# Leftover tokens of a routed mixture of experts: counting moved one batch earlier, x turned by 32x32 blocks on VectorE, their x read at the start of the last batch

## Chip, cores and metric

One core of one Trainium2 chip. The metric is the device time in microseconds (us), and the median of the runs is compared.

## The reference

Pooled attention feeds a mixture of experts in two levels. What is computed, cut to what matters:

```python
k_p = k.reshape(B, H, Sp, 8, D).mean(axis=3); v_p = v.reshape(B, H, Sp, 8, D).mean(axis=3)
attn = softmax(q @ k_p.T / sqrt(D)) @ v_p              # B=8, H=8, S=576, D=64, Sp=72
x = attn.transpose(0, 2, 1, 3).reshape(B * S, H * D)   # 4608 tokens of 512
g_idx = argmax(x @ w_group)                            # one of 4 groups, its softmax weight g_w
e_idx = argmax(x @ w_expert[g_idx])                    # one of 4 experts of it, weight e_w
out = g_w * e_w * (relu(x @ w1[g, e]) @ w2[g, e])      # w1 512x1024, w2 1024x512, float32
```

## The kernel before, in words

The kernel goes through the 8 batches one after another. Nearly all tokens of a batch choose the same expert. So each batch elects its main expert, and all its 576 tokens go through that expert; the gate of a token that chose another one is zero. Those few others, the **leftovers**, are done at the end in blocks of up to 32 slots, one expert to a block. The first block is written into the order of the last batch, and a loop behind it runs once for every further block (none in this execution).

The order of the work is written out by hand in strings, one per stage: START, FIRST (batch 0), SECOND (batch 1), STEADY (batches 2 to 6) and LAST (batch 7). Each word is one piece, and each engine takes its own instructions in the order of the words. `m.` is the expert product of the batch itself, `n.` the attention and routing of the next batch, `w.` the next batch's weights, `l.` the leftovers. The engines meet only at semaphores, which the framework places where a tile is written, read or handed on.

* `m.up:f:h` (line 602) is one slice of x @ w1 for half h of the tokens: 12 matmuls on TensorE into one of three PSUM banks (pool ps_m), and a relu on ScalarE (line 604). `m.upd` (lines 610, 615) is the VectorE part that takes the low half of the result and sets the bank free. So slice k waits for the `upd` of slice k-3.
* `m.down:z` (lines 631, 642, 663) is 8 matmuls of h @ w2. Three of these make a chunk of 128 tokens, which ScalarE scales and stores (line 636).
* `load`, `cast`, `lo` bring in a quarter of w1 (1:0 to 1:3) or of w2 (2:0 to 2:3): a DMA on SyncE's queue (line 573) into one of four buffers (pool sw), a rounding on ScalarE (line 579) and the remainder on GpSimd, or on VectorE where the word ends in `:v` (line 585). The buffer comes free after `lo`.
* `n.xlo` (line 418) is a GpSimd subtraction over x. `n.keep_x` (line 555) writes x to the DRAM tile xscr if the batch has leftovers.
* `l.step` advances the generator `place` (19 pieces) that counts the leftovers. Piece 1 makes a triangle and two constants, pieces 2 to 5 are one matmul each (line 733) into a bank of ps_t (pool of three) with a VectorE copy out of it (line 734), and the rest is short VectorE work (lines 738 to 771).
* `l.which` (lines 778 to 785) finds batch and expert of a block and has SyncE read both into registers. `l.slots` (lines 793 to 810) and `l.rows` (lines 816 to 818) find the tokens. `l.xtiles` clears two tiles on GpSimd (line 824), `l.fetch_x` (line 834), `l.fetch_a` and `l.fetch_b` read x and the expert's weights.
* `l.whole` (line 848) adds the high and low parts of x, by chunks of 128 tokens, on VectorE or GpSimd. `l.turn` (lines 858, 859) transposes a chunk on TensorE and copies it out. `l.gather` (line 866) picks the 32 tokens by a matmul with a one-hot matrix, `l.back` (line 872) transposes the result. `l.up`, `l.hback`, `l.down` (lines 880 to 899) are the expert on 32 tokens and the scattered store.

In STEADY the words that touch batches 8 and later do nothing. In batch 6, the last to use it, it ends with

```python
m.down:0 n.rt:1 x.kr:0 m.down:1 n.route m.down:2 x.kr:1 z.load_k m.down:3 m.down:4 n.main_expert w.load:1:0 w.load:1:1 w.load:1:2 w.load:1:3 m.down:5
x.qb:0 n.gates n.gm_ n.xlo:1 n.keep_x m.down:6 x.kt m.down:7 x.sc:0 x.mx:0 x.sd:0 w.cast:1:0 w.lo:1:0 w.load:2:0 m.down:8 x.ex:0 x.qb:1 w.cast:1:1 w.load:2:1 m.down:9
x.su_:0 x.nm:0:p w.lo:1:1 m.down:10 m.down:11 m.down:12 w.cast:1:2 m.down:13 w.cast:1:3
```

Of the kernel before, what the change touches and what calls it, by code (L numbers as in the profile page):

```python
# [68 lines left out]
m.load:2:3 m.load:2:2 m.up:0:0 p.tail m.upd:0:0 m.lo:1:2:v m.up:0:1 l.step m.upd:0:1 m.up:1:0 l.step l.step m.upd:1:0 m.up:1:1 l.step l.step m.upd:1:1 l.xtiles  # L69
m.up:2:0 m.cast:2:1 l.step m.upd:2:0 l.step m.up:2:1 l.step m.upd:2:1 l.step m.up:3:0 l.step l.step m.upd:3:0 m.up:3:1 l.step l.step m.upd:3:1  # L70
m.up:5:0 l.step l.step l.step l.step m.upd:5:0 m.lo:1:3 m.cast:2:2 m.up:4:0 l.step l.step l.which m.lo:2:2:v m.upd:4:0 m.lo:2:1:v
m.up:6:0 m.cast:2:0 m.upd:6:0 m.up:5:1 m.lo:2:0:v m.up:4:1 m.up:6:1 m.cast:2:3 l.fetch_x l.tiles m.upd:5:1 m.upd:4:1 m.upd:6:1 l.slots m.down:0 m.down:1 l.fetch_a:1
# [7 lines left out]
def attn_moe(ctx: ExitStack, tc: tile.TileContext, q, k, v, wg, we, w1, w2, out):  # L80
    nc = tc.nc
    tt, ts, stt = nc.vector.tensor_tensor, nc.vector.tensor_scalar, nc.vector.scalar_tensor_tensor
# [602 lines left out]
    class Left:  # L685
# [22 lines left out]
        def place(s):  # L708
# [13 lines left out]
            s.sl = [sl[:, 128 * c:128 * c + 128] for c in range(NC)]  # L722
            s.xg, s.xs, s.h = sl[:, 640:768], sl[:, 768:896], sl[:, 896:1152]
            s.hT = sl[:, 1152:1408].rearrange("p (t x) -> p t x", t=2)
            s.y = sl[:, 1408:1536]
# [94 lines left out]
        def xtiles(s):  # L820
            s.xh = [pp.tile([128, 5, S], F32, name="pT")[:, 0:NG], xp.tile([128, NG, S], F32, name="xr")]

            for t in s.xh:
                nc.gpsimd.memset(t, 0.0)
# [21 lines left out]
        def whole(s, c):  # L846
            o, n = CH[c]
            (nc.gpsimd if c % 2 else nc.vector).tensor_tensor(
                out=s.xh[0][:, :, o:o + n], in0=s.xh[0][:, :, o:o + n], in1=s.xh[1][:, :, o:o + n], op=ALU.add)

        def turn(s, c):

            if s.xr is None:
                s.xr = xp.tile([128, 2, 4, 320], F32, name="xb").rearrange("p i g s -> p (i g s)").rearrange("p (c x) -> p c x", c=NC)
            o, n = CH[c]
            ps = ps_t.tile([128, 512], F32, name="tp")
            for g in range(4):
                nc.tensor.transpose(out=ps[0:n, 128 * g:128 * g + 128], in_=s.xh[0][:, g, o:o + n], identity=ident)
            (nc.vector.tensor_copy if c % 2 else nc.scalar.copy)(out=s.xr[0:n, c, :], in_=ps[0:n])

        def gather(s):

            ps = ps_t.tile([128, 512], F32, name="tp")
            for c, (o, n) in enumerate(CH):
                for g in range(4):
                    nc.tensor.matmul(ps[32 * g:32 * g + BS, 0:128], lhsT=s.sl[c][0:n, 0:BS], rhs=s.xr[0:n, c, 128 * g:128 * g + 128],
                                     start=(c == 0), stop=(c == NC - 1))
            nc.scalar.copy(out=s.xg, in_=ps[:, 0:128])
# [132 lines left out]
```

## Time and profile before

| | us |
|---|---|
| median of 3 runs | 515.48 (514.2 to 516.41) |
| the profiled execution, its own time | 514.15 |
| its span in the trace | 512.4 |

How to read the rows further down. A row of a timeline has start, duration, engine, line, operation, output<-input, shape and how many instructions were merged; brackets tell how long the engine had been idle and what released it. PE is TensorE (PEld its weight loads), DVE VectorE, ACT ScalarE, POOL GpSimd, SPq the DMA issues of SyncE. A row of the chain has start, duration and what the end of the program hung on just then. One float32 matmul gives two instructions, a transpose one.

### The profile page before, as it was taken

What the parts mean: (1) busy time and instruction counts of PE and PEld (TensorE: products, weight loads), DVE (VectorE), ACT (ScalarE), POOL (GpSimd) and SP (SyncE); (2) the same over time, 40 slices, a digit from 0 to 9 for tenths busy, and PEclk for the clock granted to TensorE, in tenths of its full rate; (3) what the DMA queues carried; (4) which work ended last, traced back from release to release, by engine and by line L of the source; (5) the groups of instructions that cost most, each with busy time, mean ns of one, the idle gap of its engine ahead of it and who ended that gap; (6) DMA issues with size and microseconds to landing.
All of it is one profiled execution on the core that took longest, in us unless ns stands there. A gap on an engine that the chain in (4) does not pass through costs nothing.

```text
span 512.4 us, 14902 instructions
## 1 busy us (share of the span) xinstructions
PE 501.1 (98%) x6085; PEld 440.1 (86%) x6085; DVE 345.6 (67%) x928; ACT 206.3 (40%) x385; POOL 281.6 (55%) x246
## 2 busy tenths in 40 slices
PE   8899999999999999999999999999999999998996
PEld 6688987998889978899789988899789988898976
DVE  6876877899385869486784768476784764199702
ACT  2354432545216542455216551455325551344212
POOL 2386666576518595476828585476947471830400
PEclk9799999999999999999999999999999999999999
DMA  8699299685428966954197615985055100923751
GB/s 279 191 260 205 24 280 236 124 192 137 77 92 242 265 106 176 318 150 80 29 308 213 151 26 138 368 311 89 1 191 192 43 3 22 304 96 114 271 172 58
DMA packets 118110, 83.70 MB, mean 163 GB/s; under 512 B 71034, under 2 KB 93818, under 8 KB 117784
## 3 DMA queue, kind: packets, MB, share of 16 engines
q1 hardware_dynamic: 113408, 75.67, 54.7%
q10 hardware_dynamic: 4600, 7.02, 4.0%
q8 instruction: 49, 0.80, 0.7%
q14 instruction: 21, 0.17, 0.1%
q0 software_dynamic: 32, 0.04, 0.0%
HBM read 77.28 MB, written 28.53 MB: 206 GB/s over the span
## 4 chain that ended last, share of the span: by engine, by line
PE 76%; DVE 10%; DMA 5%; ACT 2%; POOL 2%; issue 2%; SPq 1%; ACTq 0%; DVEq 0%; POOLq 0%
PE mm L602 30%; PE mm L631 27%; PE mm L642 4%; PE sc L396 4%; PE sc L336 4%; DMA vv<-in_v_dram 2%; DMA sw<-in_moe_w_dram 2%; PE tp L429 1%; PE mm L663 1%; POOL w L585 1%; DVE s L368 1%; DVE ht L615 1%; DVE pT L382 1%; PE tp L425 1%; DVE p L357 1%
## 5 line engine op out<-in xcount | busy, mean ns | idle before, releaser
L631 PE MATMUL mm<-w,ht 128*128 128x512 f32 x744 | 172.6, 385 | 0.0
L585 POOL TENSOR_TENSOR w<-sw,w 128x1024 fp32r<-128x1024 f32 (+2 forms) x86 | 145.2, 1711 | 33.7 <-ACT w L579 29.2
L631 PEld LDWEIGHTS mm<-w,ht 128*128 128x128 f32 x744 | 136.8, 189 | 25.2 <-issue 6.4
L602 PE MATMUL mm<-xb,w 128*128 128x288 f32 (+1 forms) x768 | 109.6, 294 | 1.7 <-DVE ht L610 1.7
L602 PEld LDWEIGHTS mm<-xb,w 128*128 128x128 f32 x768 | 100.7, 189 | 6.1 <-ACT w L579 2.2
L602 PE MATMUL mm<-xa,w 128*128 128x288 f32 (+1 forms) x768 | 100.2, 283 | 0.5 <-ACT xa L401 0.5
L602 PEld LDWEIGHTS mm<-xa,w 128*128 128x128 f32 x768 | 95.5, 190 | 2.2 <-ACT xa L401 0.9
L604 ACT ACTIVATE ht<-mm 128x288 fp32r<-128x288 f32 (+2 forms) x128 | 51.9, 410 | 87.1 <-PE mm L602 85.4
L375 POOL TENSOR_TENSOR p<-p,su 128x864 f32<-128x864 f32 (+2 forms) x30 | 40.3, 1343 | 78.6 <-DVE su L370 67.7
L579 ACT CAST w<-sw 128x1024 fp32r<-128x1024 f32 x64 | 66.7, 1042 | 31.5 <-DMA sw<-in_moe_w_dram 29.0
L615 DVE SCALAR_TENSOR_TENSOR ht<-mm,ht 128x64 fp32r<-128x64 f32 (+4 forms) x192 | 37.7, 252 | 25.8 <-ACT ht L604 25.5
L636 ACT ACTIVATE y<-mm,gm 128x512 f32<-128x512 f32 x31 | 21.2, 684 | 66.4 <-PE mm L631 66.4
L362 ACT ACTIVATE p<-p 128x864 f32<-128x864 f32 (+2 forms) x30 | 23.4, 780 | 37.5 <-DVE p L357 29.6
L368 DVE TENSOR_REDUCE s<-p 128x12 f32<-128x864 f32 (+2 forms) x30 | 25.8, 861 | 15.1 <-ACT p L362 15.1
L382 DVE STREAM_TRANSPOSE pT<-p 128x960 f32<-128x960 f32 (+2 forms) x30 | 29.2, 972 | 8.0 <-POOL p L375 7.2
L610 DVE SCALAR_TENSOR_TENSOR ht<-mm,ht 128x288 fp32r<-128x288 f32 (+1 forms) x64 | 26.9, 422 | 10.4 <-ACT ht L604 10.4
L642 PE MATMUL mm<-w,ht 128*128 128x512 f32 x128 | 29.5, 381 | 0.0
L336 PEld LDWEIGHTS sc<-kT,qT 64*32 64x32 f32 x2176 | 23.7, 105 | 6.3 <-issue 3.5
L336 PE MATMUL sc<-kT,qT 64*32 64x72 f32 x2176 | 28.5, 229 | 0.5 <-DVE qT L322 0.2
L675 DVE TENSOR_TENSOR y<-mm,y 64x512 f32<-64x512 f32 x8 | 5.5, 682 | 33.6 <-ACT y L647 20.2
L396 PE MATMUL sc<-pT,v 32*64 32x288 f32 (+2 forms) x384 | 26.9, 409 | 0.2 <-DVE p L357 0.2
L396 PE MATMUL tp<-pT,v 32*64 32x288 f32 (+2 forms) x384 | 26.9, 409 | 0.0
(227 smaller groups left out, 568.8 us busy)
## 6 DMA issues: line engine op xcount, KB each, us to landing
sw<-in_moe_w_dram SPq DMA_DIRECT2D x72, 512.0 KB
vv<-in_v_dram SPq DMA_DIRECT2D x27, 320.0 KB
q<-in_q_dram SPq DMA_DIRECT2D x112, 72.0 KB
kv<-in_k_dram SPq DMA_DIRECT2D x14, 512.0 KB
out_dram<-y ACTq DMA_DIRECT2D x23, 256.0 KB
xscr<-xa SPq DMA_DIRECT2D x5, 1152.0 KB
xscr<-xb SPq DMA_DIRECT2D x5, 1152.0 KB
xscr<-xb SPq DMA_DIRECT2D x3, 1280.0 KB
```

Of the source, the lines that this page charges most:

```text
L336: nc.tensor.matmul(ps[x][32 * g:32 * g + 32, SP * t:SP * t + SP], lhsT=s.qT[c][64 * x:64 * x + 64, g, 32 * t:32 * t + 32], rhs=s.kT[64 * x ...
L368: red(out=two[:, :, :, 0], in_=p.rearrange("p t (x s) -> p t x s", x=2), axis=AX.X, op=ALU.add)
L375: (nc.vector if eng == "v" else nc.gpsimd).tensor_tensor(out=p, in0=p, in1=bc(s.su[c][:, 0:w], SP), op=ALU.mult)
L382: nc.vector.transpose(out=s.pT[:, :, o:o + n].rearrange("p j (t i) -> p t j i", i=32), in_=probs[:, z:z + n // 32].rearrange("p t (j i) -> ...
L396: nc.tensor.matmul(banks[a][64 * x:64 * x + 64, 0:n], lhsT=s.v6[32 * a:32 * a + 32, 5 if x and i == 0 else j, :], rhs=s.pT[32 * a:32 * a + ...
L579: nc.scalar.copy(out=s.w[m, j][0], in_=raw)
L585: (nc.vector if eng == "v" else nc.gpsimd).tensor_tensor(out=wl[:, i:i + n], in0=s.raw[m, j][:, i:i + n], in1=wh[:, i:i + n].bitcast(F32), ...
L602: nc.tensor.matmul(ps[:, 0:n], lhsT=l[:, kc, fs], rhs=apart(s.a.xt[hf][:, r, kc]), start=(kc == 0 and i == 0), stop=(kc == 3 and i == 2))
L604: nc.scalar.activation(out=halves(ht[:, sl]), in_=joined(ps[:, 0:n]), func=AF.Relu)
L615: stt(out=ht[:, at:at + hi - lo], in0=ps[:, a, lo:hi], scalar=0.0, in1=ht[:, t + lo:t + hi].bitcast(F32), op0=ALU.max, op1=ALU.subtract)
L631: nc.tensor.matmul(ps, lhsT=s.ht[f][:, 640 * l + o:640 * l + o + 128], rhs=apart(s.w[2, f // 2][r][:, f % 2, :]), start=(i == 0), stop=(i ...
L642: nc.tensor.matmul(ps, lhsT=s.ht[f][:, 512:640], rhs=apart(s.w[2, f // 2][r][:, f % 2, :]), start=(i == 0), stop=(i == 15))
```

## The change

Batch 6 gets an order of its own, PENULT, and LAST is written anew. PENULT is STEADY without the words that did nothing, but for these: the 19 counting pieces and the two clearings stand in it, and the remainders 1:0 and 1:1 go to VectorE. In LAST, `which` and `fetch_x` stand behind the first slice, ahead of the loads 2:2 and 2:3. x is turned by VectorE in 32x32 blocks, in three pieces of 192 tokens, and the picking is done by 72 matmuls on 32x32 tiles, with one-hot blocks that four further matmuls and three VectorE instructions prepare.

```diff
+PENULT = """
...
+m.down:0 n.rt:1 l.step l.xtile:0 m.down:1 n.route m.down:2 m.down:3 m.down:4 n.main_expert w.load:1:0 w.load:1:1 w.load:1:2 w.load:1:3 m.down:5
+n.gates n.gm_ n.xlo:1 n.keep_x l.xtile:1 m.down:6 m.down:7 w.cast:1:0 l.step l.step l.step l.step w.lo:1:0:v w.load:2:0 m.down:8 w.cast:1:1 l.step l.step w.lo:1:1:v w.load:2:1 m.down:9
+l.step l.step l.step m.down:10 l.step l.step l.step l.step m.down:11 l.step l.step l.step m.down:12 l.step l.step w.cast:1:2 m.down:13 w.cast:1:3
+"""
 LAST = """
...
+m.up:0:0 p.tail m.upd:0:0 l.which l.fetch_x m.lo:1:2 m.load:2:2 m.up:0:1 m.cast:2:0 m.upd:0:1 m.lo:1:3 m.load:2:3 m.up:1:0 m.upd:1:0 l.slots m.up:1:1 m.upd:1:1 m.lo:2:0
+m.up:2:0 m.cast:2:1 l.rows m.upd:2:0 m.lo:2:1:v m.up:2:1 m.upd:2:1 m.up:3:0 m.upd:3:0 m.up:3:1 m.cast:2:2 m.upd:3:1 m.up:4:0 m.upd:4:0 l.oh l.tiles l.fetch_b:1 m.up:4:1 m.upd:4:1 m.lo:2:2:v
+m.up:5:0 m.upd:5:0 l.whole:0 m.up:5:1 m.upd:5:1 l.whole:1 m.up:6:0 m.cast:2:3 m.upd:6:0 l.turn:0 m.up:6:1 m.upd:6:1 l.whole:2 m.up:7:0 m.upd:7:0 l.turn:1 m.up:7:1 m.upd:7:1 m.lo:2:3:v l.fetch_a:1
+m.down:0 l.turn:2 m.down:1 l.gather l.next_ m.down:12 l.back m.down:2 m.down:3 m.down:4 m.down:5 l.up m.down:6 l.hback m.down:7 l.down
+m.down:8 l.fetch_x l.fetch_a l.fetch_b m.down:13 m.down:9 m.down:10 l.slots m.down:11
 """
...
             nc.gpsimd.iota(s.colf, [[0, 4], [1, BS]], base=0, channel_multiplier=0, allow_small_or_imprecise_dtypes=True)
             sl = sq.tile([128, NC * DM], F32, name="q")
...
+            for k in range(4):
+                ts(out=s.sel[:, k], in0=s.colf, scalar1=float(32 * k), scalar2=rowi[:, 1:2], op0=ALU.add, op1=ALU.is_equal)
+            ts(out=s.fold, in0=s.colf[:, 0:BS], scalar1=at[:, 0, 0:1], scalar2=None, op0=ALU.is_equal)
...
-            for c in range(NC):
-                ts(out=s.sl[c], in0=s.colf, scalar1=pq[:, c:c + 1], scalar2=None, op0=ALU.is_equal)
+            tt(out=s.sl, in0=s.colf.unsqueeze(1).broadcast_to([128, NC, 128]), in1=bc(pq, 128), op=ALU.is_equal)
...
         def rows(s):
+            for k in range(4):
+                nc.tensor.matmul(mps[:, 8 + NC * k:8 + NC * k + NC], lhsT=s.sel[:, k], rhs=s.pq, start=True, stop=True)
             for c, (o, n) in enumerate(CH):
-                nc.tensor.matmul(mps[:, 0:2], lhsT=s.sl[c][0:n], rhs=s.mq[0:n, c, :], start=(c == 0), stop=(c == NC - 1))
+                nc.tensor.matmul(mps[:, 0:2], lhsT=s.sl[0:n, c], rhs=s.mq[0:n, c, :], start=(c == 0), stop=(c == NC - 1))
+
+        def oh(s):
...
+            tt(out=s.ohb, in0=s.colf[:, 0:BS].unsqueeze(1).unsqueeze(1).broadcast_to([128, 4, NC, BS]),
+               in1=bc(mps[:, 8:8 + 4 * NC].rearrange("p (k c) -> p k c", k=4), BS), op=ALU.is_equal)
+        def xtile(s, i):
+            t = xp.tile([128, NG, S], F32, name="xr") if i else pp.tile([128, 5, S], F32, name="pT")[:, 0:NG]
+            nc.gpsimd.memset(t, 0.0)
...
+        def whole(s, u):
+            z = slice(192 * u, 192 * u + 192)
+            tt(out=s.xh[0][:, :, z], in0=s.xh[0][:, :, z], in1=s.xh[1][:, :, z], op=ALU.add)
+        def turn(s, u):
+            z = slice(192 * u, 192 * u + 192)
+            nc.vector.transpose(out=s.xh[1][:, :, z], in_=s.xh[0][:, :, z])
         def gather(s):
+            for j in range(S // 32):
+                for a in range(4):
+                    r, z = slice(32 * a, 32 * a + 32), j % 4
+                    nc.tensor.matmul(banks[a][32 * z:32 * z + BS, 0:128], lhsT=s.ohb[r, j % 4, j // 4], rhs=s.xh[1][r, :, 32 * j:32 * j + 32],
+                                     start=(j < 4), stop=(j >= S // 32 - 4))
+            for i in range(2):
+                nc.scalar.copy(out=s.xg[:, :, 2 + i], in_=one[i][:, 0:128].rearrange("p (g x) -> p g x", g=NG))
+            nc.vector.tensor_copy(out=s.xg[:, :, 0:2].rearrange("p g a x -> p a g x"), in_=two[:, :, 0:128].rearrange("p a (g x) -> p a g x", g=NG))
         def back(s):
             ps = ps_t.tile([128, 512], F32, name="tp")
-            nc.tensor.transpose(out=ps[:, 0:128], in_=s.xg, identity=ident)
+            for g in range(NG):
+                nc.tensor.matmul(ps[:, BS * g:BS * g + BS], lhsT=s.xg[:, g].rearrange("p a x -> p (a x)"), rhs=s.fold, start=True, stop=True)
...
-            run(LAST if b == B - 1 else STEADY, b)
+            run(STEADY if b < B - 2 else LAST if b == B - 1 else PENULT, b)
```

## Rows read from the trace of the kernel before

**Rows 1.** The page: busy time, share of the span, instructions of each engine.
```profile
PE 501.1 (98%) x6085; PEld 440.1 (86%) x6085; DVE 345.6 (67%) x928; ACT 206.3 (40%) x385; POOL 281.6 (55%) x246
```

**Rows 2.** The chain that ended last, in order of time, from batch 6's down products.
```profile
432.35 12.13 PE mm L631 x56
...
447.93 4.41 PE mm L602 x36
452.34 0.29 PE tp L733 x2
...
477.69 1.10 PE tp L816 x10
...
478.79 1.09 PE tp L858 x8
...
481.61 0.87 PE tp L858 x8
...
485.94 0.44 PE tp L858 x4
...
488.11 1.36 PE tp L866 x40
```

**Rows 3.** Timeline of TensorE in the last batch, round its one wait.
```profile
464.53 1.63 PE L602 MATMUL mm<-xb,w 128*128 128x288 f32 x12
467.84 3.24 PE L602 MATMUL mm<-xb,w 128*128 128x288 f32 x24 [1.68 <-DVE ht L610]
```

**Rows 4.** Timeline of TensorE: the attention scores of one piece.
```profile
403.23 1.21 PE L336 MATMUL sc<-kT,qT 64*32 64x72 f32 x96
```

**Rows 5.** Timeline of GpSimd, batch 6's down products and the last batch's start.
```profile
434.46 2.64 POOL L418 TENSOR_TENSOR xb<-xr,xb 128x1152 fp32r<-128x1152 f32 x1
444.50 0.26 POOL L720 IOTA kb<- 128x128 f32 x1
446.65 2.01 POOL L824 MEMSET xr<- 128x2304 f32 x1
449.58 2.36 POOL L585 TENSOR_TENSOR w<-sw,w 128x1024 fp32r<-128x1024 f32 x1 [0.92 <-ACT w L579]
```

**Rows 6.** Timeline of ScalarE: the rounding of 1:2 in batch 6's down products.
```profile
445.69 1.05 ACT L579 CAST w<-sw 128x1024 fp32r<-128x1024 f32 x1 [0.49 <-ACT y L636]
```

**Rows 7.** Timeline of VectorE in the last batch: copies, count, which, remainder, slots.
```profile
453.45 0.87 DVE L734 COPY kv<-tp 128x320 f32<-128x320 f32 x2
457.24 0.29 DVE L738 TENSOR_TENSOR kv<-kv 128x128 f32<-128x128 f32 x1
462.79 0.82 DVE L758 SCALAR_TENSOR_TENSOR kv<-kv,loh 128x640 f32<-128x640 f32 x1
464.86 0.28 DVE L778 TENSOR_SCALAR kb<-cum,it 128x128 f32<-128x128 f32 x1
466.20 1.22 DVE L585 TENSOR_TENSOR w<-sw,w 128x1024 fp32r<-128x1024 f32 x1
472.06 0.14 DVE L793 CAST kT<-ki 128x1 f32<-128x1 int32 x1
473.69 1.06 DVE L810 TENSOR_SCALAR q<-kb,kT 128x128 f32<-128x128 f32 x5
```

**Rows 8.** One line's instructions on VectorE: duration ns min/median/max.
```profile
L543 DVE TENSOR_TENSOR gm<-gm,gate x6: 167/1282/1740, 150.6 to 436.4; 128x5 f32<-128x5 f32 x6
```

**Rows 9.** Timeline: SyncE's read of x for the leftovers, and GpSimd's wait for it.
```profile
468.66 0.36 SPq L834 DMA_DIRECT2D pT<-xscr  x1
...
477.23 3.18 POOL L848 TENSOR_TENSOR pT<-pT,xr 128x512 f32<-128x512 f32 x2 [23.83 <-DMA xr<-xscr]
```

**Rows 10.** Stretches: PE, PEld, DVE, ACT, POOL busy, granted clock, DMA share, GB/s.
```profile
15.00:20.00 5.00, 3.80 (x45) 3.24 (x42) 4.34 (x15) 1.44 (x4) 0.10 (x1) 0.77 0.31 62
20.00:25.00 5.00, 4.38 (x75) 3.66 (x76) 4.12 (x9) 3.22 (x6) 3.79 (x6) 0.54 1.01 325
...
466.00:468.00 2.00, 0.32 (x3) 0.16 (x2) 1.97 (x6) 0.48 (x2) 0.00 (x0) 1.00 0.00 0
```

More of the change, by code (lines that the diff above doesn't have):

```diff
@@ L67 @@
 """
-LAST = """
[L69 to L72, printed above, removed]
@@ L73 @@
-m.up:7:0 l.fetch_b:1 m.upd:7:0 l.whole:4 l.whole:0 m.up:7:1 l.rows l.next_ l.whole:3 m.upd:7:1 l.turn:3 l.turn:4 m.down:12
-l.whole:1 l.turn:1 l.turn:0 l.whole:2 m.lo:2:3:p m.down:2 m.down:3 l.turn:2 m.down:4 l.gather m.down:5 l.back m.down:6 l.up m.down:7 l.hback
-m.down:8 l.down l.fetch_x l.fetch_a l.fetch_b m.down:13 m.down:9 m.down:10 l.slots m.down:11
+PENULT = """
+m.up:0:0 r.cast:1:3 p.tail m.upd:0:0 n.sc:1 n.pt:0 m.lo:1:2 m.load:2:2 m.up:0:1 n.mx:1 m.upd:0:1 m.up:1:0 n.sd:1 m.lo:1:3 m.load:2:3 m.upd:1:0 n.ex:1 m.up:1:1 m.cast:2:0 m.upd:1:1 n.su_:1 n.nm:1:p
@@ new lines @@
+m.up:2:0 m.upd:2:0 n.qb:2 m.lo:2:0 m.up:2:1 m.upd:2:1 n.pt:1 m.up:3:0 n.sc:2 m.upd:3:0 m.cast:2:1 m.lo:2:1 n.mx:2 m.up:3:1 m.upd:3:1 n.sd:2
+m.up:4:0 m.upd:4:0 n.ex:2 m.up:4:1 m.upd:4:1 n.su_:2 n.nm:2:p m.up:5:0 m.upd:5:0 m.cast:2:2 m.lo:2:2 m.up:5:1 m.upd:5:1 n.pt:2
+m.up:6:0 m.upd:6:0 m.up:7:0 m.cast:2:3 m.lo:2:3 m.upd:7:0 n.av:0 n.avd:0 n.xlo:0 m.up:6:1 m.upd:6:1
+m.up:7:1 m.upd:7:1 n.av:1 n.rt:0 n.avd:1
+m.down:0 n.rt:1 l.step l.xtile:0 m.down:1 n.route m.down:2 m.down:3 m.down:4 n.main_expert w.load:1:0 w.load:1:1 w.load:1:2 w.load:1:3 m.down:5
@@ L721, in place @@
             sl = sq.tile([128, NC * DM], F32, name="q")
[L722 to L725, printed above, removed]
+            pf = probs.rearrange("p t x -> p (t x)")
+            s.sl = pf[:, 0:640].rearrange("p (c x) -> p c x", c=NC)
+            s.ohb = pf[:, 640:1280].rearrange("p (k c x) -> p k c x", k=4, c=NC)
+            s.sel = sl[:, 0:512].rearrange("p (k x) -> p k x", k=4)
+            s.xg = sl[:, 512:1024].rearrange("p (g a x) -> p g a x", g=NG, a=4)
+            s.fold, s.xs, s.h = sl[:, 1024:1056], sl[:, 1056:1184], sl[:, 1184:1440]
+            s.hT = sl[:, 1440:1696].rearrange("p (t x) -> p t x", t=2)
+            s.y = sl[:, 1696:1824]
+            for k in range(4):
+                ts(out=s.sel[:, k], in0=s.colf, scalar1=float(32 * k), scalar2=rowi[:, 1:2], op0=ALU.add, op1=ALU.is_equal)
+            ts(out=s.fold, in0=s.colf[:, 0:BS], scalar1=at[:, 0, 0:1], scalar2=None, op0=ALU.is_equal)
             s.tmp = wk.tile([128, H * SP], F32, name="kT")
@@ L800, in slots @@
             red(out=pq, in_=pb, axis=AX.X, op=ALU.add)
-            off = s.tmp[:, 56:57]
+            off = s.tmp[:, 66:67]
             ts(out=off, in0=s.it, scalar1=float(BS), scalar2=None, op0=ALU.mult)
             ts(out=pq, in0=pq, scalar1=off, scalar2=None, op0=ALU.subtract)
-            mb_ = s.tmp[:, 57:137].rearrange("p (c t b) -> p c t b", c=NC, t=2)
+            mb_ = s.tmp[:, 67:147].rearrange("p (c t b) -> p c t b", c=NC, t=2)
             tt(out=mb_, in0=s.meta.rearrange("p c b t -> p c t b"),
@@ L806, in slots @@
                in1=boh.unsqueeze(1).unsqueeze(1).broadcast_to([128, NC, 2, B]), op=ALU.mult)
-            mq = s.tmp[:, 137:147].rearrange("p (c t) -> p c t", t=2)
+            mq = s.tmp[:, 56:66].rearrange("p (c t) -> p c t", t=2)
             red(out=mq, in_=mb_, axis=AX.X, op=ALU.add)
-            for c in range(NC):
-                ts(out=s.sl[c], in0=s.colf, scalar1=pq[:, c:c + 1], scalar2=None, op0=ALU.is_equal)
-            s.mq = mq
+            tt(out=s.sl, in0=s.colf.unsqueeze(1).broadcast_to([128, NC, 128]), in1=bc(pq, 128), op=ALU.is_equal)
@@ L813, in rows @@
+            s.pq, s.mq = pq, mq
         def rows(s):
-            mps = ps_t.tile([128, 512], F32, name="tp")
+            mps = s.mps = ps_t.tile([128, 512], F32, name="tp")
+            for k in range(4):
+                nc.tensor.matmul(mps[:, 8 + NC * k:8 + NC * k + NC], lhsT=s.sel[:, k], rhs=s.pq, start=True, stop=True)
             for c, (o, n) in enumerate(CH):
-                nc.tensor.matmul(mps[:, 0:2], lhsT=s.sl[c][0:n], rhs=s.mq[0:n, c, :], start=(c == 0), stop=(c == NC - 1))
+                nc.tensor.matmul(mps[:, 0:2], lhsT=s.sl[0:n, c], rhs=s.mq[0:n, c, :], start=(c == 0), stop=(c == NC - 1))
@@ L817, in rows @@
+        def oh(s):
+            mps = s.mps
             ts(out=s.idx[:, 1:2], in0=mps[:, 0:1], scalar1=s.quarter, scalar2=None, op0=ALU.add)
             nc.vector.tensor_copy(out=s.gl[:, 1:2], in_=mps[:, 1:2])
[L820 to L824, printed above, removed]
+            tt(out=s.ohb, in0=s.colf[:, 0:BS].unsqueeze(1).unsqueeze(1).broadcast_to([128, 4, NC, BS]),
+               in1=bc(mps[:, 8:8 + 4 * NC].rearrange("p (k c) -> p k c", k=4), BS), op=ALU.is_equal)
@@ L826, in tiles @@
+        def xtile(s, i):
+            t = xp.tile([128, NG, S], F32, name="xr") if i else pp.tile([128, 5, S], F32, name="pT")[:, 0:NG]
+            nc.gpsimd.memset(t, 0.0)
+            s.xh = s.xh + [t] if i else [t]
         def tiles(s):
@@ L829, in tiles @@
             s.wb = [kv[:, 0:2], kv[:, 2:4], vv[:, 0:2], vv[:, 2:4]]
-            s.xr = None
         def fetch_x(s):
@@ L844, in fetch_b @@
                                   **({} if first else dict(cond=s.some)))
[L846 to L859, printed above, removed]
@@ L861, in gather @@
-        def gather(s):
[L863 to L868, printed above, removed]
+        def whole(s, u):
+            z = slice(192 * u, 192 * u + 192)
+            tt(out=s.xh[0][:, :, z], in0=s.xh[0][:, :, z], in1=s.xh[1][:, :, z], op=ALU.add)
@@ new lines, in turn @@
+        def turn(s, u):
+            z = slice(192 * u, 192 * u + 192)
+            nc.vector.transpose(out=s.xh[1][:, :, z], in_=s.xh[0][:, :, z])
+        def gather(s):
+            two = ps_s.tile([128, 2, 512], F32, name="sc")
+            one = [ps_t.tile([128, 512], F32, name="tp") for i in range(2)]
+            banks = [two[:, 0], two[:, 1]] + one
+            for j in range(S // 32):
[6 more added lines that the diff above has]
+            nc.vector.tensor_copy(out=s.xg[:, :, 0:2].rearrange("p g a x -> p a g x"), in_=two[:, :, 0:128].rearrange("p a (g x) -> p a g x", g=NG))
@@ L911, in block @@
             s.rows()
-            for c in range(NC):
-                s.whole(c)
-                s.turn(c)
+            s.oh()
+            for u in range(3):
+                s.whole(u)
+                s.turn(u)
+            s.gather()
             s.next_()
             s.fetch_x()
-            s.gather()
             s.back()
```

## The prediction

> **What bounds the kernel now.** I read the page's busy shares first: TensorE is busy for 98% of the span, no other engine for more than 67% [rows 1]. So the time is TensorE's work plus its waits, and another engine's work counts only where it makes TensorE wait. Then the chain that ended last, from batch 6's down products: it is TensorE almost throughout [rows 2]. The reader is to see there what the leftovers cost it: the two pairs of counting matmuls 0.29 us each, `rows` 1.10, the turning transposes 1.09 + 0.87 + 0.44 = 2.40, the gather 1.36. Last, TensorE's timeline of the last batch holds one wait: a slice of 12 matmuls starts at 464.53, and slices follow each other by 4.41 / 3 = 1.47 us [rows 2], so the next was due at 466.00 and came at 467.84, held by VectorE's low part [rows 3]. That is 1.84 us. VectorE was doing the count and the remainders just then [rows 7].
>
> The profiled execution took 514.15 us (span 512.4), 1.33 below the median of 515.48. I make the sum against it and add the difference to the median. About 0.5%, 2.6 us, is what a measurement of this kernel can tell from no change.
>
> **What goes.** The 1.84 us wait, since the count leaves the last batch, and the transposes, 2.40: together 4.24 us. That is the most there is to win.
>
> **What TensorE gets.** `rows` takes four more float32 matmuls with a 128x128 weight, eight instructions at 1.10 / 10 = 0.11 us: 0.88 [rows 2]. `back` becomes four matmuls in place of one transpose, eight instructions at 0.11 less one at 2.40 / 20 = 0.12: 0.76. The gather becomes 72 matmuls, 144 instructions, on 32x32 tiles. No row shows that form. The nearest small tiles, 64x32, were issued at 1.21 / 96 = 12.6 ns each [rows 4], which gives 144 x 12.6 = 1.8 us; the gather of before, four tiles side by side, took 1.36 / 40 = 34 ns each [rows 2], which gives 4.9. I take 1.8, the nearer in tile size, so 0.45 more than now. From below I allow 1.36, no dearer than now. Together +2.1 us. The counting matmuls move and cost the same.
>
> The Trainium skill (TensorE: Matmul & The Clock Gate, section "Wait — 56ns, not 53.3ns?") says that starts of matmuls come no closer than about 25 ns however small they are; the row of 12.6 ns disagrees, and by that floor the gather would be 3.6 us, an estimate, and the sum 1.8 us higher.
>
> Without new waits the change is therefore worth 4.24 - 2.1 = 2.1 us. So the waits decide.
>
> **First new wait: the fourth counting matmul.** In PENULT counting pieces 2 to 5 stand between down pieces 7 and 8. TensorE ends piece 7 at 432.35 + 3 x 1.733 = 437.55 (12.13 / 7 a piece) [rows 2]. Three counting matmuls run until 438.0. The fourth needs the first one's bank, for there are three, and so the first VectorE copy. In piece 2 VectorE has five small instructions ahead of that copy (four `sel`, one `fold`), which read the index tile that GpSimd writes. GpSimd comes to it late: its subtraction of x ends at 434.46 + 2.64 = 437.10, behind it now stands the clearing of tile xr, 2.01 us, until 439.1, then the index, 0.26, until 439.4 [rows 5]. Four `sel` at 1.06 / 5 = 0.21 each, `fold` at some 0.15 (between those and the 0.14 of a single element) and a copy at 0.87 / 2 = 0.44 [rows 7] end at 440.85. TensorE waits from 438.0 to 440.9: **2.9 us**, and nothing covers it, as down piece 8 is queued behind. If the clearing took half its time it would be 1.9; I see no reason for more than 3.5.
>
> **The count itself** then runs on VectorE, which then has nothing else. Copies end at 442.2, remainder 1:0 (1.22 [rows 7]) at 443.4, two pieces at 444.4. ScalarE can round 1:1 only after it has scaled the chunk of piece 8, which now ends at 442.8; for 1:2 that took 1.2 us from the end of piece 11 and the rounding 1.05 [rows 6], so here 445.05, and remainder 1:1 ends at 446.3. The last 13 pieces took from 457.24 to 464.86 before [rows 7], 7.6 us, less four low parts between, of which each took some 0.35 from them: 6.3 us, until 452.6. The four matmuls (0.58) and the wait (2.9) put the last batch's start at 447.93 + 3.5 = 451.45 [rows 2]. So `p.tail`, the low part and `which` come late on VectorE.
>
> **Second new wait: `rows`.** It stands behind slice 2:0, the fifth: 451.45 + 5 x 1.47 = 458.8 at the earliest, and needs `slots`. VectorE's instructions with both operands in SBUF stand still while a GpSimd tensor operation runs: five elements took 167 ns at best, and 1740 ns at worst [rows 8]. GpSimd's remainders, 2.36 us each [rows 5], lie just there. 1:2 follows its rounding, 2.25 us behind the end of piece 11 (448.0): 450.3 to 452.7, and holds the count's end by 0.6 us. 1:3 began 1.65 us after the down products' end [rows 5]: 453.2 to 455.55. Then VectorE does `p.tail` (512 elements, 0.7 by 0.82 for 640) and the first low part (288 elements, half a microsecond by the same row and the 0.14 of one element [rows 7]), until 454.4, and `which`, whose first instruction is held until 455.6. `which` takes 466.20 - 464.86 = 1.35 [rows 7] and ends at 457.0. Two low parts, half a microsecond each, end at 458.0. `slots` is 473.69 - 472.06 = 1.63 us and then one instruction over 640 elements in place of five, 0.82 as for the other one of that size [rows 7]: 2.45, plus some 0.95 behind remainder 2:0 on GpSimd (456.7 to 459.1): 461.5. TensorE, itself 0.3 late by then, waits until 461.6: **2.8 us** in all. With nothing held it would be 0.9.
>
> **Edits costed at nothing.** x is read some nine microseconds sooner, but TensorE never waited for it; GpSimd did [rows 9]. On SyncE's queue loads 2:2 and 2:3 now stand behind `which` and that read. It took 2.4 us from `which` to the first issue, and until 477.2, 8.5 us, to land; so x lands at about 466 to 468 and 2:2 right behind. ScalarE's rounding of 2:2 comes up at about 468, and the relus queue behind it. The new waits are its cover; without them slices 4:0 and 5:1 would feel up to 1 us. The three additions and three turns of 768 elements, about 1 us each by 0.82 for 640, stand between low parts; VectorE has the room, since half of each slice is free there. The gather waits some 0.25 us for the last turn behind remainder 2:3. Clearing pT and piece 1 run while GpSimd has nothing else to do.
>
> **Sum:** -4.24 + 2.1 + 2.9 + 2.8 + 0.25 = +3.8 us: 517.95 in the profiled sense, **519.3** against the median. Its own range, from the bounds of the waits and the gather: 517.2 to 521.5.
>
> **Rivals.** *VectorE is not late* (faster). Decided at one place: the first copy out of a counting bank. If it is done by 438.0, no bank is awaited, VectorE enters the last batch some 3 us ahead of what I laid out, and `slots` is done when `rows` comes up. Then what is left is -2.1: 513.3, or 512.3 with a gather and small matmuls that cost little. For it: only the index keeps VectorE there, 0.26 us of GpSimd. Against it: the clearing has a measured time, and the index stands behind it.
>
> *Only the bank is awaited.* The remainders on GpSimd fall between VectorE's instructions, not on them, and `rows` waits 0.9: +1.9, 517.4. For it: some of those five-element instructions were not held at all [rows 8]. Against it: three remainders of 2.36 us in 9 us leave little between.
>
> *The gather's tiles run four side by side*, as those of before: 3.1 more, 522.4.
>
> *TensorE's clock falls in the first new wait.* From 15 to 20 us, where TensorE was busy for 3.80 of 5 us, the granted clock fell from 1.00 (2.4 GHz) to 0.50 (1.2 GHz); over those and the next five it was 0.77 and 0.54 on the mean [rows 10]: 5 x 0.23 + 5 x 0.46 = 3.4 us lost: 522.7. Against it: round the 1.84 us wait it stayed at 1.00 [rows 10]. The Trainium skill (the same page, section "What's actually happening") has the low level as the default that activity lifts; the rows from 15 to 25 us agree.
>
> **How the numbers follow.** Forecast 0.42, only the bank 0.25, VectorE not late 0.20, slow gather 0.07, clock 0.06. Faster by over 0.5% (below 512.9) is the lower part of the rival that needs cheap matmuls too: 0.12. Slower (above 518.1): 0.33 of the forecast, 0.07 of the bank alone, and the two dear ones: 0.53. Same: 0.35. The range leaves out the two dear ends above and half of the fast rival below: 513.0 to 521.8.
>
> **What would show it.** Right: TensorE idle for about 3 us between down pieces 7 and 8, released by the VectorE copy of line 734's kind, with GpSimd's clearing ending just before the first `sel`; and idle again in the last batch ahead of `rows`, released by VectorE's 640-element instruction. `which` and a part of `slots` drawn out under GpSimd's remainders. The gather in 1.8 us. No transposes of x on TensorE and no wait where 1.68 stood. Wrong: the fourth counting matmul right behind the third, or `rows` right behind its slice.

## The result, and the profile after

The changed kernel takes 520.6 us (median of 6 runs, 519.2 to 524.1); the kernel before, beside it on the same chip, 514.84. The ratio is 1.0127 [1.0097, 1.0156]: slower by 1.3%. The forecast was 519.3.

The profiled execution is the longest of the six, 524.1 us (span 522.3). It came to down piece 2 of batch 6, ahead of everything that was changed, at 430.21 us, where the kernel before was at 426.74. These 3.5 us are not put down to the change: in the seven experiments the same piece came between 425.24 and 428.51, and about half of them is the granted clock of the first 60 us, 0.91 against 0.94 (60 x 0.03 = 1.8). So I measure one **stretch** in each trace: from the start of that piece to the start of the last 48 matmuls of down products (line 671, before 663). It was 502.61 - 426.74 = 75.9 us and is 512.55 - 430.21 = 82.3: 6.5 us more.

The changed kernel's page, busy time and share of the span by engine, answers [rows 1]: TensorE does more and is still the bound.

```profile
PE 507.6 (97%) x6184; PEld 445.8 (85%) x6184; DVE 352.0 (67%) x929; ACT 205.0 (39%) x383; POOL 276.6 (53%) x243
```

The changed kernel's timeline of TensorE, where the counting matmuls now stand and where `rows` does (start, duration, group; in brackets the idle time and what ended it):

```profile
440.88 0.61 PE L748 MATMUL tp<-loh,v 128*128 128x320 f32 x3
444.38 0.41 PE L748 MATMUL tp<-loh,v 128*128 128x320 f32 x1 [2.88 <-DVE kv L749]
...
456.67 1.63 PE L610 MATMUL mm<-xa,w 128*128 128x288 f32 x12
...
462.72 1.71 PE L610 MATMUL mm<-xa,w 128*128 128x288 f32 x12
465.61 1.06 PE L830 MATMUL tp<-kT,q 128*128 128x5 f32 x8 [1.18 <-DVE kT L818]
466.75 1.36 PE L832 MATMUL tp<-kT,p 128*128 128x2 f32 x10
468.05 2.58 PE L610 MATMUL mm<-xb,w 128*128 128x288 f32 x12
470.42 2.50 PE L610 MATMUL mm<-xa,w 128*128 128x288 f32 x12
472.76 1.63 PE L610 MATMUL mm<-xb,w 128*128 128x288 f32 x12
```

Three things are to be seen. The wait of [rows 3] is gone. The fourth counting matmul waits 2.88 us for the first copy. `rows` begins 465.61 - 462.72 = 2.89 us after the slice ahead of it, 1.42 more than a slice takes. And there is a third: the two slices behind `rows` are 2.37 and 2.34 us apart, with no wait in them. The changed kernel's stretches of that time, with the columns of [rows 10] (the granted clock stands behind the five engines), say why:

```profile
444.00:446.00 2.00, 1.62 (x5) 1.41 (x6) 2.00 (x5) 0.00 (x0) 0.41 (x3) 0.72 1.09 347
446.00:448.00 2.00, 2.00 (x6) 1.56 (x5) 1.54 (x5) 0.00 (x0) 0.00 (x0) 0.50 0.34 86
448.00:450.00 2.00, 2.00 (x10) 1.70 (x10) 0.00 (x0) 1.56 (x2) 0.00 (x0) 0.93 0.78 252
...
468.00:470.00 2.00, 2.00 (x13) 1.98 (x13) 0.69 (x1) 0.00 (x0) 0.00 (x0) 0.69 1.03 428
470.00:480.00 10.00, 10.00 (x75) 10.00 (x75) 5.15 (x17) 3.41 (x7) 0.00 (x0) 0.89 1.02 387
```

Behind each of the two waits the granted clock fell from 1.00 (2.4 GHz) to 0.50 (1.2 GHz) for a while. Behind the bank wait that cost 2 x 0.28 + 2 x 0.50 + 2 x 0.07 = 1.7 us, behind `rows` 2 x 0.31 + 10 x 0.11 = 1.7.

The changed kernel's timeline of GpSimd, then that of VectorE; they answer to [rows 5] and [rows 7]:

```profile
440.65 2.02 POOL L843 MEMSET xr<- 128x2304 f32 x1
442.62 0.25 POOL L728 IOTA kb<- 128x128 f32 x1
...
455.70 5.14 POOL L593 TENSOR_TENSOR w<-sw,w 128x1024 fp32r<-128x1024 f32 x2 [11.30 <-ACT w L587]
462.08 2.37 POOL L593 TENSOR_TENSOR w<-sw,w 128x1024 fp32r<-128x1024 f32 x1 [1.24 <-ACT w L587]
```

```profile
442.91 0.87 DVE L739 TENSOR_SCALAR q<-kb,rowi 128x128 f32<-128x128 f32 x4 [1.82 <-POOL kb L728]
443.84 1.67 DVE L749 COPY kv<-tp 128x320 f32<-128x320 f32 x4
...
450.20 1.23 DVE L593 TENSOR_TENSOR w<-sw,w 128x1024 fp32r<-128x1024 f32 x1 [2.63 <-ACT w L587]
...
457.08 1.39 DVE L775 TENSOR_SCALAR pos<-pos 128x40 f32<-128x40 f32 x1
...
459.62 1.31 DVE L793 TENSOR_SCALAR kb<-cum,it 128x128 f32<-128x128 f32 x1
...
462.92 1.56 DVE L810 TENSOR_SCALAR kT<-desc 128x8 f32<-128x8 f32 x1
...
465.88 0.81 DVE L824 TENSOR_TENSOR p<-kb,kT 128x640 f32<-128x640 f32 x1
```

The clearing stands ahead of the index tile, VectorE sits idle for it, then writes `sel`, and only then copies. Later three of VectorE's small instructions end just as a remainder on GpSimd does: the one at 457.08 and the one at 459.62 under the pair (455.70 to 460.84), the one at 462.92 under remainder 2:0 (462.08 to 464.45). Two of these three remainders, 1:2 and 2:0, were VectorE's in the kernel before (`lo:1:2:v` and `lo:2:0:v`); the new LAST gave them to GpSimd, as 1:0 and 1:1 went to VectorE.

The changed kernel's chain that ended last, in order of time, round the gather; it answers to [rows 2]:

```profile
489.61 0.23 PE sc L882 x2
...
491.72 1.92 PE mm L650 x8
493.65 0.81 PE tp L891 x8
```

The gather's 144 instructions take 491.72 - 489.61 = 2.11 us, and `back` 0.81.

The stretch by its terms: wait -1.84, transposes -2.40, `rows` 2.39 - 1.19 = +1.20 (from its start to the next group's, in experiments 4 and 5 further down: 2.39 the new one where it neither waits nor loses clock, 1.19 the old one), gather 2.11 - 1.36 = +0.75, `back` 0.81 - 0.11 = +0.70, bank wait +2.88, waits at `rows` +1.6 (1.42, 0.17 in the slices ahead, and 0.05 in `rows` itself, 468.05 - 465.61 against 2.39), clock +3.4. Sum **+6.3**, measured 6.5.

### The profile page after: what moved, and what is told of

It is laid out like the page before. It is cut to its first block, busy times and chain, and to the rows that moved or that the text cites. A ratio compares the mean times of both kernels' runs of the same rounds, so it can differ in the third digit from the quotient of the medians.

```text
span 522.3 us, 15093 instructions
## 1 busy us (share of the span) xinstructions
PE 507.6 (97%) x6184; PEld 445.8 (85%) x6184; DVE 352.0 (67%) x929; ACT 205.0 (39%) x383; POOL 276.6 (53%) x243
## 4 chain that ended last, share of the span: by engine, by line
PE 71%; DVE 12%; DMA 6%; POOL 4%; ACT 2%; issue 2%; SPq 1%; ACTq 0%; DVEq 0%; POOLq 0%
PE mm L610 28%; PE mm L639 26%; PE sc L344 4%; PE sc L404 3%; PE mm L650 3%; DMA vv<-in_v_dram 3%; DMA sw<-in_moe_w_dram 2%; PE tp L437 1%; PE mm L671 1%; DMA pT<-in_k_dram 1%; POOL w L593 1%; DVE p L365 1%; DVE s L376 1%; DVE mx L356 1%; DVE ht L623 1%
## 5 line engine op out<-in xcount | busy, mean ns | idle before, releaser
L593 POOL TENSOR_TENSOR w<-sw,w 128x1024 fp32r<-128x1024 f32 (+2 forms) x85 | 143.2, 1707 | 44.5 <-ACT w L587 44.4
L639 PEld LDWEIGHTS mm<-w,ht 128*128 128x128 f32 x744 | 138.2, 191 | 25.5 <-issue 6.2
L610 PE MATMUL mm<-xb,w 128*128 128x288 f32 (+1 forms) x768 | 112.8, 300 | 0.0
L610 PEld LDWEIGHTS mm<-xb,w 128*128 128x128 f32 x768 | 103.5, 193 | 4.3 <-ACT w L587 2.2
L610 PE MATMUL mm<-xa,w 128*128 128x288 f32 (+1 forms) x768 | 101.5, 285 | 0.5 <-ACT xa L409 0.5
L650 PEld LDWEIGHTS mm<-w,ht 128*128 128x128 f32 x128 | 24.0, 189 | 3.5 <-issue 0.2
```

The source lines that it names most:

```text
L593: (nc.vector if eng == "v" else nc.gpsimd).tensor_tensor(out=wl[:, i:i + n], in0=s.raw[m, j][:, i:i + n], in1=wh[:, i:i + n].bitcast(F32), ...
L610: nc.tensor.matmul(ps[:, 0:n], lhsT=l[:, kc, fs], rhs=apart(s.a.xt[hf][:, r, kc]), start=(kc == 0 and i == 0), stop=(kc == 3 and i == 2))
L639: nc.tensor.matmul(ps, lhsT=s.ht[f][:, 640 * l + o:640 * l + o + 128], rhs=apart(s.w[2, f // 2][r][:, f % 2, :]), start=(i == 0), stop=(i ...
L650: nc.tensor.matmul(ps, lhsT=s.ht[f][:, 512:640], rhs=apart(s.w[2, f // 2][r][:, f % 2, :]), start=(i == 0), stop=(i == 15))
```

## The experiments

Two theories stood against each other. **A**: two new waits of TensorE make it slower, each with its own cause (the index tile behind the clearing; VectorE held by GpSimd's remainders ahead of `rows`), and the clock's fall follows from them. **B**: the new way of turning is dearer by itself, or the clock falls whatever is done about the waits. All ratios are to the kernel before on the same chip. "Clock" is the mean granted clock over all timed runs (before: 0.998); it takes in the whole execution, also the first 60 us, whose clock lay between 0.91 and 1.00 in the nine traces. "By terms" is worked out below.

| kernel | median us (runs) | ratio [95%] | clock | stretch us | by terms |
|---|---|---|---|---|---|
| changed | 520.6 (6) | 1.0127 [1.0097, 1.0156] | 0.991 | 82.3 | 82.2 |
| 1 index early | 517.17 (10) | 1.0056 [1.0033, 1.0078] | 0.993 | 79.7 | 79.7 |
| 2 filler at the bank | 520.28 (5) | 1.0101 [1.0067, 1.0135] | 0.991 | 80.8 | 80.6 |
| 3 remainder 2:0 later | 518.64 (5) | 1.0082 [1.0053, 1.0111] | 0.994 | 80.9 | 80.6 |
| 4 all together | 513.74 (10) | 0.9982 [0.995, 1.0013] | 0.997 | 75.0 | 74.8 |
| 5 counting moved alone | 512.37 (12) | 0.9968 [0.9945, 0.9991] | 0.997 | 74.4 | 74.5 |
| 6 rounding early | 522.43 (4) | 1.015 [1.0089, 1.021] | 0.989 | 85.9 | 86.2 |
| 7 index early, filler at rows | 515.87 (12) | 1.0038 [1.0014, 1.0062] | 0.997 | 76.8 | 76.5 |

**1. The index tile early.** The index, `sel` and `fold` are written in the counting's first piece, ahead of the clearing of xr.

```
 def count piece 1:
+    nc.gpsimd.iota(s.colf, ...)
+    ... sel, fold ...
     nc.gpsimd.affine_select(out=tri, ...)
...
 def count piece 2:
-    nc.gpsimd.iota(s.colf, ...)
-    ... sel, fold ...
```

> The index tile, the four sel and fold are made in counting piece 1, ahead of GpSimd's subtraction and clearing; nothing else moves. Theory W (the new waits make it slower): the fourth counting matmul now waits only for the first copy, 0.2 us in place of 2.88, and down piece 8 starts about 2.7 us sooner; the wait ahead of rows stays between 1 and 2 us, since VectorE still waits for the rounding of 1:1. Theory C (the granted clock falls behind a wait): the fall behind the counting matmuls goes too, 1.7 us more in runs that have it. So 2.7 to 4.4 us off the changed kernel's 520.6. Rival (TensorE's own extra work makes it slower): no change beyond 0.5 us.

TensorE's timeline of experiment 1, and its stretches behind `rows`:

```profile
437.89 0.41 PE L748 MATMUL tp<-loh,v 128*128 128x320 f32 x1 [0.28 <-DVE kv L749]
...
457.71 1.16 PE L830 MATMUL tp<-kT,q 128*128 128x5 f32 x8 [1.28 <-DVE kT L818]
```

```profile
456.00:460.00 4.00, 2.72 (x18) 2.43 (x16) 3.83 (x14) 1.34 (x2) 0.55 (x1) 0.82 0.72 214
460.00:464.00 4.00, 4.00 (x18) 3.97 (x18) 0.80 (x1) 0.00 (x0) 0.00 (x0) 0.50 0.98 403
464.00:468.00 4.00, 4.00 (x29) 4.00 (x29) 1.04 (x4) 0.90 (x3) 0.00 (x0) 0.83 1.04 392
```

The bank wait is gone, so the index tile was its cause, and the median falls by 3.4 us. VectorE did not come earlier to `rows`, which still waits, and here its clock costs 4 x 0.18 + 4 x 0.50 + 4 x 0.17 = 3.4. Terms: 82.3 - 2.6 (the wait) - 1.7 + 1.7 (clock gone at the one, more at the other) = 79.7.

**2. Filler in the bank wait.** Six matmuls of ones, whose result nobody reads, stand ahead of the fourth counting matmul; the rest of the computation is unchanged.

```
-... w.cast:1:0 l.step l.step l.step l.step w.lo:1:0:v ...
+... w.cast:1:0 l.step l.step l.step t.warm:6 l.step w.lo:1:0:v ...
```

> Six matmuls of ones, whose result nobody reads, stand ahead of the fourth counting matmul, 2.6 us of TensorE work in its 2.88 us wait; all else as in the changed kernel. Theory C: the granted clock stays at 1.00 behind them, and the time falls by up to 1.7 us in runs that had the fall. Theory W alone: the wait is the same length but filled, the time is the same within 0.5 us, and the clock behind the last batch's wait may still fall.

TensorE's timeline of experiment 2 and a stretch behind the wait:

```profile
439.62 2.75 PE L967 MATMUL mm<-ones 128*128 128x256 f32 x12
442.69 0.42 PE L748 MATMUL tp<-loh,v 128*128 128x320 f32 x1 [0.31 <-DVE kv L749]
```

```profile
444.00:448.00 4.00, 4.00 (x20) 3.50 (x19) 2.81 (x6) 1.73 (x2) 0.00 (x0) 1.00 0.48 110
```

The copy comes as late as it did; TensorE was only kept busy, and in the trace its clock then stayed at 1.00 there. The stretch is 1.5 us shorter, about the clock's 1.7 (terms: 82.3 - 1.7 = 80.6). The medians do not show it (520.28 and 520.6), nor do the mean clocks, so over many runs this one stays open.

**3. Remainder 2:0 later.** Its rounding and its subtraction on GpSimd move from behind slices 0:1 and 1:1 to behind slice 2:1.

```
-... m.up:0:1 m.cast:2:0 m.upd:0:1 ... m.up:1:1 m.upd:1:1 m.lo:2:0
+... m.up:0:1 m.upd:0:1 ... m.up:1:1 m.upd:1:1
-... l.rows m.upd:2:0 m.lo:2:1:v m.up:2:1 m.upd:2:1 ...
+... l.rows m.upd:2:0 m.lo:2:1:v m.up:2:1 m.cast:2:0 m.lo:2:0 m.upd:2:1 ...
```

> The rounding of 2:0 on ScalarE, and with it GpSimd's remainder 2:0, comes three slices later; nothing else moves. Theory L (a GpSimd tensor operation holds VectorE's instructions): the second instruction of slots takes 0.2 us in place of 1.56, and the wait ahead of rows shrinks by 1.3 us, to 0.3 or less. Rival (slots is late only because the count is late): the instruction is held by something else or the wait stays at 1.2 to 1.7 us. The bank wait stays at 2.9.

VectorE's timeline of experiment 3, then TensorE's, ScalarE's, and two stretches:

```profile
457.95 0.16 DVE L810 TENSOR_SCALAR kT<-desc 128x8 f32<-128x8 f32 x1
```

```profile
459.30 1.00 PE L830 MATMUL tp<-kT,q 128*128 128x5 f32 x8
...
469.14 1.63 PE L610 MATMUL mm<-xa,w 128*128 128x288 f32 x12
472.08 1.74 PE L610 MATMUL mm<-xb,w 128*128 128x288 f32 x12 [1.30 <-DVE ht L618]
```

```profile
470.18 1.04 ACT L587 CAST w<-sw 128x1024 fp32r<-128x1024 f32 x1 [3.37 <-DMA sw<-in_moe_w_dram]
```

```profile
460.00:464.00 4.00, 3.91 (x32) 3.79 (x31) 2.43 (x7) 1.39 (x3) 0.00 (x0) 1.00 0.97 311
...
472.00:476.00 4.00, 3.92 (x32) 3.92 (x33) 4.00 (x12) 1.22 (x4) 0.00 (x0) 1.00 1.05 378
```

The eight-element instruction takes 0.16 us where it took 1.56: it was GpSimd's subtraction that held it. `rows` no longer waits, and behind it the clock stays at 1.00. But slice 5:1 now starts 2.94 us after the one ahead, 1.47 late: the rounding of 2:2 waits for its load, which is queued behind the read of x. Terms: 82.3 - 1.5 (the waits at `rows`; the 0.17 in the slices ahead stays) - 1.7 (the clock) + 1.47 = 80.6.

**4. Both, with the loads ahead of x.** Experiments 1 and 3, the rounding of 1:1 ahead of down piece 8, and loads 2:2 and 2:3 issued ahead of `which` and the read of x.

```
-... w.load:2:0 m.down:8 w.cast:1:1 l.step ...
+... w.load:2:0 w.cast:1:1 m.down:8 l.step ...
-m.up:0:0 p.tail m.upd:0:0 l.which l.fetch_x m.lo:1:2 m.load:2:2 m.up:0:1 ... m.lo:1:3 m.load:2:3 m.up:1:0 ...
+m.up:0:0 p.tail m.upd:0:0 m.lo:1:2 m.load:2:2 m.lo:1:3 m.load:2:3 l.which l.fetch_x m.up:0:1 ... m.up:1:0 ...
```

> Index early as in e1, remainder 2:0 late as in e3, the rounding of 1:1 ahead of the scaling of down piece 8's chunk, and loads 2:2 and 2:3 issued ahead of which and the read of x. Theory W: both waits go (under 0.5 us each), so does the fall of the clock, and what is left is the balance of work: 1.84 of wait and 2.40 of transposes less, 0.9 for rows, 0.7 for back and 0.7 for the gather more: about 2 us faster than the kernel before, 512 to 514. Rival (the change's work on VectorE makes it the bound of the last batch): slices wait for low parts, and the time stays above the kernel before.

TensorE's timeline of experiment 4, and one of its stretches:

```profile
439.11 0.41 PE L748 MATMUL tp<-loh,v 128*128 128x320 f32 x1 [0.29 <-DVE kv L749]
...
457.32 1.01 PE L830 MATMUL tp<-kT,q 128*128 128x5 f32 x8
...
459.71 1.74 PE L610 MATMUL mm<-xb,w 128*128 128x288 f32 x12
```

```profile
446.00:466.00 20.00, 19.90 (x148) 19.11 (x147) 15.37 (x48) 10.18 (x17) 7.09 (x3) 1.00 0.63 234
```

No wait over 0.3 us is left, `rows` takes 459.71 - 457.32 = 2.39 us, and the clock stays. Without its waits the change is worth 75.9 - 75.0 = 0.9 us in the trace, less than the 2.1 of the prediction, and its ratio's interval holds 1: no change that can be measured. Terms: 82.3 - 2.6 - 1.5 - 3.4 = 74.8, as 0.29 of the wait at the fourth counting matmul and the 0.17 in the slices ahead of `rows` stay.

**5. The counting moved alone.** The kernel before with its own `rows`, turning on TensorE, gather and `back`; only the counting, the clearing and the read of x are moved as in experiment 4, and the last batch's list is written anew round them.

```
+PENULT = """ ... as in experiment 4 ... """
-run(LAST if b == B - 1 else STEADY, b)
+run(STEADY if b < B - 2 else LAST if b == B - 1 else PENULT, b)
```

> The count alone: the kernel before with the counting pieces and clearings in batch 6 as in e4 (rounding of 1:1 early, loads ahead of the read of x), the read of x early, and turn, gather, rows and back as they were, on TensorE and with transposes. Theory W with the balance of work as e4's trace shows it (transposes 2.40 less; rows 1.29, back 0.70, gather 0.75 more, so 0.34 more in sum): the wait of 1.84 goes and nothing new comes, 1.3 to 1.9 us faster than the kernel before and about 0.3 to 0.8 faster than e4. Rival (turning on VectorE is what made e4 no slower than before): e5 is slower than e4.

TensorE's timeline of experiment 5:

```profile
473.87 1.26 PE L824 MATMUL tp<-kT,q 128*128 128x2 f32 x10
475.06 1.09 PE L865 MATMUL tp<-ident,pT 128*128 128x128 f32 x8
```

Turning costs TensorE what it did before, and TensorE nowhere waits longer than 0.3 us. With 12 and 23 runs the interval of its ratio leaves out 1, narrowly. Its median and its stretch are the lowest of all kernels here; by terms the stretch is 75.9 - 1.84 + 0.3 + 0.17 = 74.5, with the two small waits that experiment 4 keeps as well. Turning by VectorE with the gather on small tiles gains nothing over the transposes; by the traces it loses 0.6 us against this version. The medians, 512.37 and 513.74, agree in sign, but the intervals of the two ratios overlap.

**6. Only the rounding early.** The changed kernel with the rounding of 1:1 ahead of down piece 8 and nothing else.

```
-... w.load:2:0 m.down:8 w.cast:1:1 l.step ...
+... w.load:2:0 w.cast:1:1 m.down:8 l.step ...
```

> The changed kernel with only the rounding of 1:1 ahead of the scaling of down piece 8's chunk. Theory W: VectorE's idle time of 2.63 us ahead of remainder 1:1 goes, the count ends over 2 us sooner, slots is done before GpSimd's remainder 2:0 begins, and the wait ahead of rows (1.2 us) goes; as in e3 slice 5:1 then waits about 1.3 us for the late load 2:2. The bank wait stays at 2.9. 518 to 520. Rival (only GpSimd's remainder 2:0 makes the wait): it stays above 1 us.

A miss. VectorE's timeline of experiment 6, GpSimd's beside it, and TensorE's:

```profile
455.55 1.69 DVE L793 TENSOR_SCALAR kb<-cum,it 128x128 f32<-128x128 f32 x1
...
457.98 2.14 DVE L798 CAST ki<-kT 128x2 int32<-128x2 f32 x1
```

```profile
454.79 2.38 POOL L593 TENSOR_TENSOR w<-sw,w 128x1024 fp32r<-128x1024 f32 x1 [0.41 <-ACT w L587]
457.74 2.35 POOL L593 TENSOR_TENSOR w<-sw,w 128x1024 fp32r<-128x1024 f32 x1 [0.58 <-ACT w L587]
```

```profile
457.38 1.63 PE L610 MATMUL mm<-xb,w 128*128 128x288 f32 x12
461.01 2.67 PE L610 MATMUL mm<-xa,w 128*128 128x288 f32 x12 [1.99 <-DVE ht L623]
```

```profile
462.00:470.00 8.00, 8.00 (x37) 7.97 (x36) 3.70 (x11) 1.34 (x2) 0.00 (x0) 0.50 0.81 300
```

VectorE's idle 2.63 us is gone and the count ends sooner, but `which` now starts under remainder 1:3 and its two-element cast under 2:0: 2.14 us in place of 0.17. The low part behind it is late, and slice 2:0 waits. The wait has moved one place up, and the clock's fall behind it is the longest of all: from 460 to 472 us some 2 x 0.10 + 8 x 0.50 + 2 x 0.46 = 5.1. Terms: 82.3 - 1.6 + 2.16 (461.01 - 457.38 - 1.47) + 3.4 (5.1 - 1.7) = 86.2.

**7. Filler ahead of `rows`.** Experiment 1 with three matmuls of ones ahead of `rows`, their result again read by nobody.

```
-... m.cast:2:1 l.rows m.upd:2:0 ...
+... m.cast:2:1 t.warm:3 l.rows m.upd:2:0 ...
```

> e1 with three matmuls of ones, read by nobody, ahead of rows: 1.3 us of TensorE work in the wait of 1.28. Theory C: the granted clock stays at 1.00 behind rows, where e1's profile lost 3.4 us at 0.50, and the median falls by up to 3.4 us, to 514 to 516. Rival (what the clock loses behind rows is not the wait's doing, or is lost elsewhere in the runs that were only timed): the time stays at e1's 517.2 within 0.7 us.

TensorE's timeline of experiment 7, and a stretch of it:

```profile
456.66 1.46 PE L967 MATMUL mm<-ones 128*128 128x256 f32 x6
458.09 1.05 PE L830 MATMUL tp<-kT,q 128*128 128x5 f32 x8
```

```profile
460.00:470.00 10.00, 10.00 (x81) 9.91 (x81) 3.86 (x13) 3.23 (x7) 0.00 (x0) 1.00 1.02 397
```

`rows` starts as late as in experiment 1, and the clock stays at 1.00: the stretch is 2.9 us shorter (terms: 79.7 - 3.4 + 0.2, as two later slices take 1.57 and 1.58 for 1.47), the median 1.3, and the mean clock over the timed runs is 0.997 against 0.993. So in the trace the clock's fall behind `rows` is a cost of its own, which goes when TensorE is kept busy there. Over the runs it is likely but not shown, since the intervals of the two ratios overlap; the clocks of experiment 1's runs (0.990 to 0.997) suggest that not every run pays it in full.

Theory A holds: each wait goes with its cause, and with both gone so is the loss. In the traces the clock fell behind the bank wait wherever that stood (changed, 3, 6) and nowhere else there, and behind the wait at `rows`, or at the slice ahead of it, wherever one stood unfilled (changed, 1, 2, 6) and nowhere else there; each trace is one execution. Of B one part holds: the new way is no cheaper for TensorE.

## Why the prediction came out as it did

**What goes**: right, 4.24 us; no wait stands where the 1.68 was.

**What TensorE gets**: 1.20 + 0.75 + 0.70 = 2.65 in place of 2.1. `back` cost 0.70 (0.76 expected). The gather's instructions came 2.11 us / 144 = 14.6 ns apart, not 12.6; the row of 64x32 tiles was the right neighbour, and the one of 34 ns was far off. The Trainium skill's floor of about 25 ns between starts (TensorE: Matmul & The Clock Gate, "Wait — 56ns, not 53.3ns?") does not hold for these 32x32 tiles either. The addition to `rows` was priced at 0.88 and cost 1.20. At 0.88 the extra work would have been 2.33, just under the 2.40 of the transposes that it replaces; at 2.65 it is dearer than they.

**The bank wait**: 2.9 expected, 2.88 measured, with clearing, index, `sel` and copy in the order laid out.

**The count's end and `slots`**: the last instruction of `slots` was laid out to end 461.5 - 451.45 = 10.05 us after the last batch's start; it ended 466.69 - 456.67 = 10.02 after it. The holds fell on a tensor_scalar of 40, of 128 and of 8 elements, as remainder after remainder ran. The Trainium skill (SBUF — State Buffer, "Who interferes with whom") counts tensor_scalar and cast among the VectorE operations that, in their two-port modes, can be shut out by a GpSimd instruction for that one's whole length; here 1.56 against 0.16 us and 2.14 against 0.17 agree.

**The wait at `rows`**: 2.8 expected, 1.6 measured. The step that failed is "needs `slots`". Only the five old matmuls need its last instruction; the four new ones need the sums of line 818 and ran, 1.1 us of them, while VectorE wrote the 640 elements. 2.8 - 1.1 = 1.7 is left, close to the 1.6.

**The clock**: it was a rival, to come in the place of the forecast, at 3.4 us and with 0.06. It came on top of the forecast, behind both waits, 1.7 each. The argument against it was the 1.84 us wait of before, round which the clock stayed [rows 10]. That wait lay between full slices; behind the new ones came five- and two-column matmuls, or TensorE stood still for 2.88 us; which of these differences matters, no run here shows. This is the largest wrong term. With the other terms as measured the sum is -4.24 + 2.65 + 2.88 + 1.64 = +2.9, 517.8 over the 514.84 beside it, and 521.2 with the whole 3.4; 520.6 lies between, and the mean granted clock of the timed runs, 0.991 against 0.998, suggests that most of them lost some. That the forecast came within 1.3 us is in part luck. Two errors were of opposite sign, 1.2 too much at `rows` and the clock left out. And the change was forecast at +3.8 us from a base of 515.48, where it is +5.8 from 514.84, so that 0.6 of the 2.0 us of error is hidden by the base.

**The gather's wait** of 0.25 for the last turn did not show: the last turn ended at 489.24, before the down piece ahead did (489.61). **x**: no slice waited for loads 2:2 and 2:3 in the changed kernel, and with the waits at `rows` gone (experiment 3) one did by 1.47 us, half as much again as was named for that case (up to 1 us).

## What to carry to other kernels

Before moving a block of work on an in-order queue, write down what it lands in front of on every queue: here a clearing of 2 us that was free in its old place delayed an index tile of 0.25 us, and TensorE stood for 2.9. Price a wait of the matrix engine with the clock behind it: in the profiled execution two waits of 2.9 and 1.6 us were followed by another 3.4 us lost at the lower clock. And take apart a change of several ideas: moving the counting, with its clearing and the read of x, was worth 514.29 - 512.37 = 1.9 us by the medians (1.5 in the traces), and in the changed kernel two new waits, the clock behind them and a new way of turning and gathering that was no cheaper hid it.
